# Attention and two mixtures on one core: a shorter lead of the maxima and earlier products with v in the opening

## The chip, the cores and the metric

The kernel runs on one core of a Trainium2 chip. The metric is the device time of one execution in microseconds, from the runs' times; a profile of one execution shows where that time goes. Engines are called TensorE (PE in the rows; PEld is its weight load), VectorE (DVE), ScalarE (ACT), GpSimd (POOL) and SyncE (SP, which issues DMAs).

## What is computed

Two batches of eight heads with 768 positions and 64 columns each. The scores of a pair of positions count only where both fall into the same of 64 buckets, given by the signs of six projections.

```python
q_bits = (np.einsum('bhsd,dk->bhsk', q, proj) > 0)
k_bits = (np.einsum('bhsd,dk->bhsk', k, proj) > 0)
mask = q_bucket[:, :, :, None] == k_bucket[:, :, None, :]
scores = np.where(mask, scale * np.matmul(q, k.transpose(0, 1, 3, 2)), -1e9)
scores = scores - np.max(scores, axis=-1, keepdims=True)
attn = np.exp(scores); attn = attn / (np.sum(attn, axis=-1, keepdims=True) + 1e-09)
return np.matmul(attn, v)
```

The result goes through a first mixture (1536 tokens, 512 columns, 2048 inner) and a second one with eight experts, one of which is chosen for each token. The change touches the attention only.

## The kernel before

Sixteen heads are taken one after the other, numbered 0 to 15 across both batches. For each head k and q are split into a high and a low f16 part ("hi" on ScalarE, "lo" on VectorE, or on GpSimd for heads 2 and 3), turned into the tile "tx" (keys and queries with columns on the partitions), projected (`args`, tile "ar"), and the signs written as "bits" beside a copy of the high part ("dup") into the tile "kq", which is turned in its turn into "tm". Heads 0 to 3 are turned by TensorE: twelve transposes into two PSUM buffers (`turn_pe`, tiles "psx0/1", "psm0/1"), and two copies `cx0`, `cx1` or `cm0`, `cm1` by ScalarE or VectorE (letters a, d). From head 4 on SP's transposing DMAs do that (`turn_in`).

A head's row maxima come before its scores. `max_unit` multiplies a query tile of 128 rows with 512 keys (c=0) or two query tiles with the other 256 keys (c=1) into one PSUM buffer "ms", and VectorE reduces it (lines 411 and 412, 415 and 416); nine such units make a head. `max_end` (lines 424, 425) joins them. For heads 0 to 3 `rows_t` turns the result by six small transposes into "tm" in PSUM, and `rows_in` copies it as a row into the operand of the scores (line 436).

A score unit (`score_unit`, lines 451 and 453) handles one key tile of 128 keys against 768 queries: two matmuls on tx, then two on tm, which needs the row of maxima. ScalarE takes the exponential into "p" (line 456). The products with v (`pv`) run in two halves for each key tile, in float32 (line 478) or, for the key tiles 2 and 5 of heads from 2 on, as three f16 matmuls (line 471). `out` copies the sum out.

PSUM is divided in three pools of two buffers each: ps_s for scores, ps_o for the sums of pv (and some early operands), and ps_m for everything else: ms, ar, tm, psx and psm from key tile 0 on, "tpe" (the turned expert embedding), and one buffer of the first mixture at the end. A buffer is given to the next tile when the last reader of its tile is done.

`run_all` writes the order out by hand; every engine follows the program's order. A list `PRO` gives the prologue. Then a loop goes over key tiles g from G0 = -2 to 101, with six positions in each. Score unit t of head n stands at g = 6n + t; its pv follows PVL = 3 key tiles later; the maxima lead by MXL = 10 key tiles, three units for each two key tiles. In the opening S0 and O0 give the key tiles of head 0's score units and pv. The table AT places the other steps by positions relative to the head's first key tile, AT3 those of head 3. At the end of each key tile `hook(g)` issues a share of the first mixture's preparation: weight loads on SP from g = -2, their conversion from key tile 5 on ("cv" on VectorE, then ScalarE and GpSimd), the embedding's steps ("emb": tpe at the end of key tile 11, its copy "enT" at the end of 12).

In the opening before, TensorE has in this order: head 0's row, score 0, two maxima of head 1, head 2's turned operand (into ps_o), score 1, four maxima, score 2, maxima, head 3's turned operand, and head 0's pv only in key tile 2, after the fifth score unit; head 1's maxima are complete one key tile earlier and head 2's begin in the same one.

Of the kernel before, what the change touches and what calls it, by code (L numbers as in the profile page):

```python
# [22 lines left out]
NJ = S // P  # L23
# [17 lines left out]
AT = dict(rows_t=-7, rows_in=-7, m_row=-22, bits=-90, max_end=-25, hi=-150, lo0=-127, lo1=-122, dup=-114, in_x=-116, in_m=-84, args=-91, load_kq=-182, load_v=-37, out0=50, out1=54, s_row=55, inv=77, r_out=79, r_in=91, scale=116, v16=18, p16=(9, 13), xhi=127, xlo=139)  # L41
# [6 lines left out]
SP, MP, OP = 1, (1, 5, 11), (1, 5)  # L48
# [3 lines left out]
XAT = 1, 9  # L52
TX, NX = (1, 3), {(14, 3): 0, (15, 1): 1, (15, 3): 0}
NPE = 4
AT3 = dict(x=-105, cx0=-105, cx1=-104, args=-94, m=-76, cm0=-75, cm1=-75, bits=-93, dup=-117)
CP3 = ("dd", "ad")
PVL, MXL = 3, 10
DUPE = "a"
G0 = -2
S0, O0 = (None, None, -1, 1, 2, 3), (2, 3, 4, 5, 7, 8)  # L60
PRO = """
hi 0 0
hi 0 1
# [59 lines left out]
bits 2  # L123
bits 2
score_unit 0 0
max_unit 1 0 0
hi 4
max_unit 1 1 0
m 2 o
score_unit 0 1  # L130
cm 2 1 d
cm 2 0 a
max_unit 1 1 1
""".split("\n")[1:-1]
KQW, NATW = 768, 832

# [13 lines left out]
class Attn:  # L150
# [396 lines left out]
    def run_all(self, bs, hook=None):  # L547

        seq = [(b, h) for b in bs for h in range(H)]
        N = len(seq)  # L550

        self.load_kq(0, 2)
        self.load_v(0, 0)
        act, dve = self.nc.scalar.copy, self.nc.vector.tensor_copy
        Z, pools, copies, its = self.Z, dict(s=self.ps_s, o=self.ps_o, m=self.ps_m), dict(a=act, d=dve), {}
        for line in PRO:
            f, *x = line.split()
            b, h = seq[int(x[0])] if x and f[:4] != "warm" else (0, 0)
            if f == "warm":
                self.warm(int(x[0]))  # L560
            elif f == "warm_s":
                self.warm(int(x[0]), self.ps_s.tile([P, 2, 512], F32, tag="s", name="warmed")[:, 0, 0:HS])
            elif f == "proj":
                self.proj()
            elif f == "kq":
                self.load_kq(b, h)
            elif f in ("x", "m"):
                (self.out_x if f == "x" else self.out_m)(b, h, self.turn_pe, pools[x[1]], x[1])
            elif f in ("cx", "cm"):
                Z[b, h][f](int(x[1]), copies[x[2]])  # L570
            elif f == "dup":
                self.dup(b, h, copies[x[1]])
            elif f == "args":
                self.args(b, h, pools["o"] if x[1] == "o" else None, *(int(y) for y in x[2:]))
            elif f in ("bits", "max_end"):
                if (f, h) not in its:
                    its[f, h] = getattr(self, f)(b, h)
                next(its[f, h], None)
            else:
                getattr(self, f)(b, h, *(int(y) for y in x[1:]))  # L580
        todo = {}

        def put(n, at, f, *args):
            todo.setdefault(n * NJ * 6 + at, []).append(partial(f, *seq[n], *args))

        def steps(n, f, *ats):
            def one(b, h):
                it.append(it.pop() if it else f(b, h))
                next(it[0], None)

            it = []
            for at in ats:
                put(n, at, one)

        for n in range(N):
            for name, at in AT.items():
                if n == 3:
                    at = AT3.get(name, at)
                if n == N - 1 and name in LAST:
                    continue  # L600
                if n < FROM.get(name, 0) or n >= UNTIL.get(name, N) or n % EVERY.get(name, (1, 0))[0] != EVERY.get(name, (1, 0))[1]:
                    continue
                if name == "p16":
                    for t in T16:
                        for u in range(2):
                            put(n, 6 * t + at[u], self.p16, t, u)
                elif name in GAP:
                    d = GAP[name]
                    steps(n, getattr(self, name), *(at + i * d for i in range(STEPS[name])))
                elif name == "dup":  # L610
                    put(n, at, self.dup, copies[DUPE])
                elif name in ("lo0", "lo1"):
                    put(n, at, self.lo, int(name[2]))
                elif name in ("in_x", "in_m"):
                    put(n, at, self.turn_in, name[3])
                else:
                    put(n, at, getattr(self, name))
        put(N - 2, XAT[0], self.extra)
        for n, t in NX:
            put(n, 6 * t + XAT[1], self.px, t)  # L620
        for k, f in (("x", self.out_x), ("m", self.out_m)):
            put(3, AT3[k], f, self.turn_pe, self.ps_m, "m")
            for i in range(2):
                copy = copies[CP3[k == "m"][i]]
                put(3, AT3[f"c{k}{i}"], lambda b, h, k, i, copy: Z[b, h]["c" + k](i, copy), k, i, copy)
        put(3, AT3["dup"], self.dup, dve)
        for g in range(G0, TEND + 1):
            n, t = divmod(g, NJ)
            m, j = divmod(g + MXL, NJ)
            p, u = divmod(g - PVL, NJ)  # L630
            if g < NJ:
                n, t = (0, S0.index(g)) if g in S0 else (-1, 0)
            if g < PVL + NJ:
                p, u = (0, O0.index(g)) if g in O0 else (-1, 0)
            for pos in range(6):
                first = g >= NJ + PVL and 0 <= p < N and u == NJ - 1
                if pos == SP and first:
                    self.pv(*seq[p], u, 0)
                    self.out(*seq[p], 0)
                if pos == SP and 0 <= n < N and not first:  # L640
                    self.score_unit(*seq[n], t)
                late = g == NJ - 1 and pos == OP[1]
                if late:
                    self.pv(*seq[p], u, 1)
                if 0 <= m < N and j % 2 * 6 + pos in MP:
                    i = MP.index(j % 2 * 6 + pos)
                    self.max_unit(*seq[m], j // 2 * 2 + (i > 0), int(i == 2))
                if pos == SP and 0 <= n < N and first:
                    self.score_unit(*seq[n], t)
                if pos in OP and 0 <= p < N and not (first and pos == OP[0]) and not late:  # L650
                    self.pv(*seq[p], u, OP.index(pos))
                for f in todo.get(6 * g + pos, ()):
                    f()
            if hook:
                hook(g)
# [849 lines left out]
```

## Time and profile before

| | us |
|---|---|
| median of 3 runs | 672.34 |
| lowest, highest | 672.31, 672.40 |
| profiled execution | 672.12 |
| span of the profiled execution, first to last instruction | 670.3 |
| TensorE busy in the span | 654.1 |
| VectorE, ScalarE busy | 467.5, 481.7 |

The profile is of one execution, and times in the rows are microseconds from the start of its span. A busy TensorE counts each matmul from its start to the modelled end, which includes draining. The clock granted to TensorE was 0.995 of full speed in the mean.

### The profile page before, as it was taken

To read this page: it belongs to the slowest core of one execution; us is meant where nothing else is said; L and a number is where in the kernel's file an instruction comes from. 1 tells how busy PE (TensorE), PEld (TensorE's weight loads), DVE (VectorE), ACT (ScalarE), POOL (GpSimd) and SP (SyncE) were. 2 spreads that over 40 slices of the span, in tenths; PEclk is the share of its full clock that TensorE was granted. 3 is DMA by queue.
4 is the path that set the end of the run, shared out by engine and by line. 5 is a ranking of instruction groups with operands and counts; after the bars stand their busy time and mean duration, and the time that the engine had idled before them with its cause. 6 is when DMAs were issued, how large, how long until landed. Compare 5 with 4: busy or idle time off the path is not lost.

```text
span 670.3 us, 10658 instructions
## 1 busy us (share of the span) xinstructions
PE 654.1 (98%) x3947; PEld 376.5 (56%) x3947; DVE 467.5 (70%) x795; ACT 481.7 (72%) x731; POOL 173.8 (26%) x244
## 2 busy tenths in 40 slices
PE   7999999999999999999999999999999999999994
PEld 4555555556555544444444544445477777667772
DVE  7867899999998868899655565545565765556620
ACT  6567788788776888889999788987754665555530
POOL 4023033122223422232353242532431011101111
PEclk9999999999999999999999999999999999999998
DMA  8155677977753323349033030310446988987500
GB/s 246 40 137 147 149 184 132 226 150 161 161 123 88 88 64 103 110 116 278 0 98 91 1 127 24 75 28 1 162 175 196 340 251 268 271 245 256 172 24 22
DMA packets 118429, 92.72 MB, mean 138 GB/s; under 512 B 85444, under 2 KB 97732, under 8 KB 118370
## 3 DMA queue, kind: packets, MB, share of 16 engines
q1 hardware_dynamic: 110242, 80.65, 45.0%
q0 software_dynamic: 2240, 6.31, 2.8%
q10 hardware_dynamic: 5888, 5.01, 2.4%
q8 instruction: 33, 0.54, 0.4%
q14 instruction: 26, 0.21, 0.1%
HBM read 63.44 MB, written 14.24 MB: 116 GB/s over the span
## 4 chain that ended last, share of the span: by engine, by line
PE 85%; DVE 8%; ACT 3%; issue 1%; DMA 1%; POOL 0%; POOLq 0%; ACTq 0%; DVEq 0%
PE x L930 15%; PE h L871 14%; PE y L1273 12%; PE h L1259 12%; PE o L478 11%; PE s L453 4%; PE s L451 4%; PE o L471 4%; PE ms L411 3%; PE ms L415 1%; DVE mx L412 1%; DVE cv L799 1%; PE ar L319 1%; DVE w L974 1%; DVE mx L416 1%
## 5 line engine op out<-in xcount | busy, mean ns | idle before, releaser
L871 PE MATMUL h<-xx,wi 128*128 128x512 f16 x576 | 131.3, 379 | 0.4 <-DVE w L956 0.3
L930 PE MATMUL x<-wo,g 128*128 128x512 f16 x576 | 131.2, 379 | 0.0
L478 PE MATMUL o<-p,vn 128*65 128x384 f32 (+3 forms) x260 | 104.3, 486 | 0.4 <-DVE su L503 0.4
L456 ACT ACTIVATE p<-s 128x768 f32<-128x768 f32 x96 | 77.2, 807 | 34.0 <-PE s L453 33.1
L930 PEld LDWEIGHTS <-g 128*128 128x128 f16 x576 | 56.2, 98 | 68.1 <-POOL g L968 0.8
L871 PEld LDWEIGHTS <-wi 128*128 128x128 f16 x576 | 56.0, 98 | 67.5 <-issue 0.9
L968 POOL TENSOR_TENSOR g<-w,g 128x512 f16<-128x512 f32 x47 | 57.4, 1221 | 135.4 <-ACT g L967 85.6
L1273 PE MATMUL y<-b,hh 128*128 128x512 f16 (+1 forms) x384 | 84.2, 379 | 0.0
L1259 PEld LDWEIGHTS <-a 128*128 128x128 f16 x768 | 75.1, 98 | 5.1 <-issue 0.2
L412 DVE TENSOR_REDUCE mx<-ms 128x1 f32<-128x512 f32 x96 | 64.9, 687 | 10.0 <-PE ms L411 9.3
L1259 PE MATMUL h<-xt,a 128*128 128x240 f16 x672 | 70.0, 266 | 0.0
L974 DVE SCALAR_TENSOR_TENSOR w<-w,u 128x512 f32<-128x512 f32 x47 | 34.4, 733 | 49.0 <-ACT u L965 46.8
L1273 PEld LDWEIGHTS <-hh 128*128 128x128 f16 (+1 forms) x384 | 43.7, 114 | 37.6
L951 DVE SCALAR_TENSOR_TENSOR t<-t,u 128x512 f32<-128x512 f32 x47 | 33.7, 718 | 28.8 <-ACT t L980 28.8
L1283 POOL DMA_INDIRECT out_dram<-o,row x16 | 16.5, 1034 | 142.6 <-ACT o L1280 98.8
L745 DVE SCALAR_TENSOR_TENSOR b<-st,b 128x1024 f16<-128x1024 f32 x28 | 33.1, 1222 | 25.5 <-ACT b L744 25.5
L478 PEld LDWEIGHTS o<-p,vn 128*65 128x65 f32 (+1 forms) x260 | 40.2, 163 | 16.2 <-issue 6.9
L745 DVE SCALAR_TENSOR_TENSOR a<-st,a 128x1024 f16<-128x1024 f32 x28 | 34.3, 1225 | 20.6 <-ACT a L744 20.6
L453 PE MATMUL s<-tm 97*128 97x384 f16 x192 | 47.0, 325 | 0.2 <-DVE tm L436 0.2
L451 PE MATMUL s<-tx 128*128 128x384 f16 x192 | 46.8, 325 | 0.0
L1280 ACT ACTIVATE o<-y,row 128x512 f32<-128x512 f32 (+2 forms) x16 | 10.8, 672 | 44.1 <-PE y L1273 28.2
L1265 ACT ACTIVATE hh<-h 128x480 f16<-128x480 f32 x32 | 18.2, 570 | 33.1 <-PE h L1259 30.3
(218 smaller groups left out, 1081.5 us busy)
## 6 DMA issues: line engine op xcount, KB each, us to landing
st<-in_moe_w_dram SPq DMA_DIRECT2D x32, 1024.0 KB, 5.5
stg<-in_moe_w_in_dram SPq DMA_DIRECT2D x16, 512.0 KB, 5.0
stg<-in_moe_w_out_dram SPq DMA_DIRECT2D x16, 512.0 KB, 4.2
xs<-zrow SPq DMA_DIRECT2D x15, 257.0 KB, 5.9
vn<-in_v_dram SPq DMA_DIRECT2D x16, 192.0 KB, 5.5
rb<-rd SPq DMA_DIRECT2D x14, 192.0 KB, 4.5
xr<-row SPq DMA_DIRECT2D x2, 1024.0 KB, 5.6
kq<-in_k_dram ACTq DMA_DIRECT2D x5, 384.0 KB, 5.4
```

The costliest lines, as they stand in the source:

```text
L412: nc.vector.tensor_reduce(z["mx"][:, j, 0:1], s, axis=AX.X, op=ALU.max)
L451: nc.tensor.matmul(s[:, c, :], kq[:, 0, ts], kq[:, 1, c * HS : (c + 1) * HS], start=True, stop=False)
L453: nc.tensor.matmul(s[:, c, :], m[0:97, 0, ts], m[0:97, 1, c * HS : (c + 1) * HS], start=False, stop=True)
L456: nc.scalar.activation(p[:, 0:S].rearrange("p (c n) -> p c n", c=2), s, AF.Exp, scale=2.0**-11)
L478: nc.tensor.matmul(o, self.vn(b, h, t), z["p"][t][:, cs], start=(t == 0), stop=(t == NJ - 1))
L745: nc.vector.scalar_tensor_tensor(lo, src, sc, hi, op0=ALU.mult, op1=ALU.subtract)
L871: self.nc.tensor.matmul(h, self.wi[wu][:, k, fs], x[:, k, xs], start=(i == 0), stop=(i == 3 * NKT - 1))
L930: nc.tensor.matmul(x2[r], gf[:, gu, rs], self.wo[wu][:, f, :], start=(f == 0 and gu + wu == 0), stop=(f == NF1 - 1 and gu == 1))
L968: nc.gpsimd.tensor_tensor(g[G - 1][:, 1, :], p1, g[G - 1][:, 0, :], op=ALU.subtract)
L974: nc.vector.scalar_tensor_tensor(w, w, 1.0, u, op0=ALU.add, op1=ALU.mult)
L1259: nc.tensor.matmul(h[:, v, :], W[0][wu][:, k, fs], xt[e][:, xu * NKT + k, :], start=(i == 0), stop=(i == 3 * NKT - 1))
L1273: nc.tensor.matmul(y[s][0 : CS[s].stop - CS[s].start], hs[F // 2][:, hu, F % 2, CS[s]], W[1][wu][:, F, :], start=(F == 0 and hu + wu == 0) ...
```

## The change

The lead of the maxima falls from ten to eight key tiles. Where MXL gave unit j of head m at g = 6m + j - 10, a list of the units of heads 1 to 15 is now taken from, one for each key tile from g = -2 on and two in the key tiles 12 and 17 (TWO), after which the lead is ten again. Head 0's six score units stand at prologue, prologue, -2, -1, 0 and 1 in place of prologue, prologue, -1, 1, 2 and 3, and its pv at -2, -1, 1, 3, 5 and 7 in place of 2, 3, 4, 5, 7 and 8. Head 2's operand tm is turned in key tile 2 through ps_m, not in the prologue through ps_o; head 3's goes from key tile 4 to key tile 8. The steps of `max_end` move to 13 positions ahead of heads 1 and 2, and 19 ahead of head 3.

```diff
-AT3 = dict(x=-105, cx0=-105, cx1=-104, args=-94, m=-76, cm0=-75, cm1=-75, bits=-93, dup=-117)
+AT3 = dict(x=-105, cx0=-105, cx1=-104, args=-94, m=-58, cm0=-57, cm1=-57, bits=-93, dup=-117, max_end=-19)
+AT12 = dict(max_end=-13)
-PVL, MXL = 3, 10
+PVL, TWO = 3, (12, 17)
-S0, O0 = (None, None, -1, 1, 2, 3), (2, 3, 4, 5, 7, 8)
+S0, O0 = (None, None, -2, -1, 0, 1), (-2, -1, 1, 3, 5, 7)
@@ PRO
 score_unit 0 0
-max_unit 1 0 0
-hi 4
-max_unit 1 1 0
-m 2 o
 score_unit 0 1
-cm 2 1 d
-cm 2 0 a
-max_unit 1 1 1
@@ run_all
-                if n == 3:
-                    at = AT3.get(name, at)
+                at = (AT12 if n < 3 else AT3 if n == 3 else AT).get(name, at)
...
-        for k, f in (("x", self.out_x), ("m", self.out_m)):
-            put(3, AT3[k], f, self.turn_pe, self.ps_m, "m")
+        for n, k, f in ((3, "x", self.out_x), (2, "m", self.out_m), (3, "m", self.out_m)):
+            put(n, AT3[k], f, self.turn_pe, self.ps_m, "m")
...
-                put(3, AT3[f"c{k}{i}"], lambda b, h, k, i, copy: Z[b, h]["c" + k](i, copy), k, i, copy)
+                put(n, AT3[f"c{k}{i}"], lambda b, h, k, i, copy: Z[b, h]["c" + k](i, copy), k, i, copy)
+        maxima = [(m, j) for m in range(1, N) for j in range(NJ)]
         for g in range(G0, TEND + 1):
             n, t = divmod(g, NJ)
-            m, j = divmod(g + MXL, NJ)
+            mj = [maxima.pop(0) for _ in range(1 + (g in TWO)) if maxima]
...
-                if 0 <= m < N and j % 2 * 6 + pos in MP:
-                    i = MP.index(j % 2 * 6 + pos)
-                    self.max_unit(*seq[m], j // 2 * 2 + (i > 0), int(i == 2))
+                for m, j in mj:
+                    if j % 2 * 6 + pos in MP:
+                        i = MP.index(j % 2 * 6 + pos)
+                        self.max_unit(*seq[m], j // 2 * 2 + (i > 0), int(i == 2))
```

Written out, the new order is this. A number stands for the head; "max" is one maximum unit, "pv a" and "pv b" the two halves of a product; steps of other engines are given where they read a buffer of ps_m or stand between such steps on VectorE; "cv" is the weight conversion at the key tile's end.

```
end of PRO: row of 0, score 0, score 1
-2: score 2; max 1; 0 pv a; dup 3 (VectorE); max 1; 0 pv b
-1: hi 4 (ScalarE); score 3; 0 pv a; max 1; 0 pv b
 0: score 4; max 1; psx0, psx1 of 3 (copies on VectorE); max 1
 1: score 5; 0 pv a; max 1; 0 pv b
 2: max 1; ar of 3; psm0, psm1 of 2; bits 3; cm0 (ScalarE), cm1 (VectorE); bits 3; max 1; bits 3; lo 4
 3: 0 pv a; lo 4; max 1; 0 pv b; max_end 1
 4: max 2; max 2; row of 1
 5: dup 4, hi 5 (ScalarE); 0 pv a, b; max 2; cv
 6: 1 score 0; max 2; max 2
 7: 1 score 1; 0 pv a; max 2; 0 pv b; cv
 8: 1 score 2; max 2; out of 0 (ScalarE); psm0, psm1 of 3; cm0, cm1; max 2; ar of 4; lo 5; cv
 9: bits 4; 1 score 3; 1 pv a; bits 4; lo 5; max 2; 1 pv b; max_end 2; cv
10: 1 score 4; max 3; 1 pv a; max 3; 1 pv b; row of 2
11: dup 5, hi 6 (ScalarE); 1 score 5; 1 pv a; max 3; 1 pv b; tpe; cv
12: 2 score 0; max 3; 1 pv a; max 3; max 3; 1 pv b; enT (VectorE); cv
13: 2 score 1; max 3; 1 pv a; max 3; 1 pv b
14: 1 pv a; out of 1; 2 score 2; max 3; 1 pv b; max_end 3; ar of 5; lo 6; cv
15: bits 5; 2 score 3; max 4; 2 pv a; bits 5; lo 6; max 4; 2 pv b; cv
16: 2 score 4; 2 pv a; low part of p (VectorE); max 4; 2 pv b; row of 3
17: 2 score 5; max 4; 2 pv a; max 4; max 4; 2 pv b; cv
```

From key tile 18 on the order is that of before.

## Rows read from the trace of the kernel before

**Rows 1.** The page: TensorE's share, and the chain that ended last by engine.
```profile
PE 654.1 (98%) x3947; PEld 376.5 (56%) x3947; DVE 467.5 (70%) x795; ACT 481.7 (72%) x731; POOL 173.8 (26%) x244
...
PE 85%; DVE 8%; ACT 3%; issue 1%; DMA 1%; POOL 0%; POOLq 0%; ACTq 0%; DVEq 0%
```

**Rows 2.** Table by stretch: length, busy us per engine, clock, DMA share, GB/s.
```profile
17.40:25.00 7.60, 6.11 (x49) 3.64 (x48) 6.94 (x14) 5.93 (x10) 0.28 (x1) 1.00 0.05 16
25.00:36.40 11.40, 11.23 (x74) 5.84 (x73) 8.11 (x18) 5.66 (x8) 0.90 (x1) 1.00 0.41 83
36.40:46.70 10.30, 10.30 (x60) 5.49 (x59) 9.07 (x21) 4.86 (x7) 3.45 (x3) 1.00 0.36 97
```

**Rows 3.** Timeline of TensorE, opening: start, us, engine, line, operation, idle before.
```profile
18.14 0.48 PE L453 MATMUL s<-tm 97*128 97x384 f16 x2 [0.22 <-DVE tm L436]
...
21.39 0.38 PE L411 MATMUL ms<-tm 96*128 96x512 f16 x1 [0.57 <-DVE mx L416]
...
22.96 0.38 PE L411 MATMUL ms<-tm 96*128 96x512 f16 x1 [0.32 <-DVE mx L412]
23.56 1.09 PE L253 MATMUL psx<-ident,ka 128*128 128x128 f16 x12 [0.22 <-DVE mx L416]
24.70 0.38 PE L411 MATMUL ms<-tm 96*128 96x512 f16 x1
24.92 0.49 PE L451 MATMUL s<-tx 128*128 128x384 f16 x2
...
25.57 0.38 PE L415 MATMUL ms<-tm 96*128 96x256 f16 x2
...
26.66 0.81 PE L478 MATMUL o<-p,vn 128*65 128x384 f32 x2
27.31 0.45 PE L319 MATMUL ar<-pj,tx 128*128 128x18 f16 x12
```

**Rows 4.** Timeline of TensorE, later stretches.
```profile
33.71 0.83 PE L253 MATMUL psm<-ident,kq 128*128 128x128 f16 x12
34.38 0.81 PE L478 MATMUL o<-p,vn 128*65 128x385 f32 x2
35.19 0.38 PE L415 MATMUL ms<-tm 96*128 96x256 f16 x2
...
36.39 0.59 PE L411 MATMUL ms<-tm 96*128 96x512 f16 x2 [0.17 <-ACT tm L255]
...
49.97 0.38 PE L411 MATMUL ms<-tm 96*128 96x512 f16 x1
...
51.13 0.38 PE L411 MATMUL ms<-tm 96*128 96x512 f16 x1
...
84.39 0.45 PE L319 MATMUL ar<-pj,tx 128*128 128x18 f16 x12 [0.49 <-DVE mx L412]
```

**Rows 5.** Timeline of VectorE, the same columns.
```profile
20.65 0.69 DVE L416 TENSOR_REDUCE mx<-ms 128x2 f32<-128x512 f32 x1
...
29.03 1.02 DVE L291 SCALAR_TENSOR_TENSOR ka<-kq,ka 128x384 f16<-128x384 f32 x2
...
50.38 0.69 DVE L412 TENSOR_REDUCE mx<-ms 128x1 f32<-128x512 f32 x1 [0.62 <-PE ms L411]
...
52.15 0.18 DVE L854 COPY enT<-tpe 128x64 f16<-128x64 f16 x1
```

**Rows 6.** Timeline of ScalarE, the same columns.
```profile
18.67 0.81 ACT L456 ACTIVATE p<-s 128x768 f32<-128x768 f32 x1 [0.40 <-PE s L453]
...
35.54 0.80 ACT L255 COPY tm<-psm 128x768 f16<-128x768 f16 x1
```

**Rows 7.** Waits of TensorE, whole span: total us, times, longest.
```profile
PE o L478 <- DVE su L503: 0.4, 1, 0.4
...
PE h L871 <- DVE w L956: 0.3, 1, 0.3
```

**Rows 8.** DMA issues from 25 to 60 us: count, median us to landing.
```profile
tx<-ka SPq DMA_TRANSPOSE x3, 3.8
```

## The prediction, made before the changed kernel ran

> **What bounds the kernel now.** I read first the totals of the engines: TensorE is busy 98% of the span and the chain that ended last is 85% TensorE [rows 1]. A kernel like that gains or loses time where TensorE stands still. Then the table by stretch [rows 2]: from 25 us on TensorE is nearly full in every stretch, while in the opening, from 17.40 to 25.00 us, it is busy for 6.11 of 7.60 us and VectorE for 6.94. So in that stretch VectorE sets the pace, and the change is aimed there. Third, TensorE's own timeline there [rows 3] and further on [rows 4], with VectorE's and ScalarE's beside it [rows 5, 6].
>
> A busy share hides part of a wait, because a matmul's record includes the time in which it drains. I therefore count issue time, the distance between starts in an unbroken run: 0.65 us for a score unit (24.92 to 25.57), 0.22 for a maximum's matmul (24.70 to 24.92; its record of 0.38 holds 0.16 of draining), 0.65 for one half of a product with v (26.66 to 27.31), 0.67 for twelve transposes (33.71 to 34.38) and 0.30 for the projections "ar" (0.45 less the draining) [rows 3, 4]. What exceeds this between two starts is a wait; where the row shows idle time, the wait is that and the 0.16.
>
> **How a wait comes about.** Each maximum, projection, "tm" row and half of a transposed operand takes one of two PSUM buffers of the pool ps_m and holds it until VectorE or ScalarE has read it. The case to learn from: the matmul at 49.97 ends 0.38 later, its reduction starts at 50.38 and lasts 0.69, and the next maximum starts at 51.13 in the same buffer, because the other one is held by "tpe" until its copy at 52.15 [rows 4, 5]. One buffer turns round in 1.16 us. TensorE runs in the order of the program, so everything behind such a matmul waits too, products and scores included. Two allocations in a row cost nothing; the third needs 1.16 us of other work since the first, or it waits.
>
> **Part 1: what goes.** The waits of before from the first score on are 0.39 (score, for the tm row), 0.72 (at 21.39), 0.49 (22.96), 0.38 (23.56) and 0.47 (inside the twelve transposes that take 1.14 in place of 0.67) [rows 3], then 0.12 (the projections at 27.31 end late), 0.16 (35.19), 0.32 (36.39) and 0.29 (51.13) [rows 4]. That is 3.34 us. Only the first is sure to remain: the first score unit doesn't move. The greatest possible gain is 2.95 us.
>
> **Part 2: the new order.** The amount of work is unchanged: the same matmuls, reductions and copies, and the listing shows the lead made up by two doubled key tiles, 12 and 17, after which the orders are equal. So only waits count. I carry TensorE's, VectorE's and ScalarE's queues forward in the new order, with these durations and 0.05 us from the end of a reader to the start of the matmul that waited for it (reduction at 20.65, and 0.69, makes 21.34; matmul at 21.39) [rows 3, 5].
>
> Key tiles -2 to 1. The three scores come at once, and the third needs the buffer that the first exponential (18.67 + 0.81 = 19.48) frees [rows 6]: it could start at 19.13, so 0.40 of wait. Then maxima and products alternate and no maximum waits. In key tile 0 there is no product: the second half of head 3's transposes waits for the reduction of the maximum just ahead (0.60), and the next maximum for the copy of the first half (0.20). TensorE reaches the end of key tile 1 at 28.8 us with 0.39 + 0.40 + 0.60 + 0.20 = 1.59 of waits, where before had 2.57 up to the same time. To here the change gains 1.0 us.
>
> Key tile 2. Neither a score nor a product lies in it; it has five allocations in a row: maximum, ar, two halves of head 2's operand (which before took two buffers of another pool), maximum. They wait 0.07 for a reduction, 0.57 for the next one, 0.04 for the reading of ar, and the last 0.70 for ScalarE's copy, which takes 0.80 [rows 6]. Sum 1.38.
>
> Key tiles 3 and 4. VectorE now has in one run the late maximum, the end of the bits, the two "lo" parts of head 4 (1.02 for two), the last maximum of head 1, the two small steps of its end and head 2's first maximum [rows 5]. By my count the last maximum of head 1 is reduced at 34.1 and head 2's first at 35.1, while TensorE has nothing left but maxima and the tm row from 33.3 on: 0.84 and 0.77, sum 1.61.
>
> Key tiles 6 and 8. In 6 it waits 0.07. In 8 a score and then five allocations: 0.60 for the second half of head 3's operand and 0.82 for the maximum behind it, as ScalarE has an exponential and an output copy ahead of its copy. Sum 1.49.
>
> Key tiles 9 to 17. The tm row of head 2 waits 0.42 for head 3's first maximum, which stands behind maximum end and weight work on VectorE. Then tpe holds one buffer through key tile 12, as before; but 12 is now a doubled tile, with three maxima on the one that is left: 0.29 for the second, as before, and 0.94 for the third, which follows the second at once. In 15 it is 0.05, in 17 (doubled too) 0.26. Sum 1.96.
>
> The new waits are 1.59 + 1.38 + 1.61 + 1.49 + 1.96 = 8.03 us, against 3.34: **+4.7 us**. From key tile 18 on nothing differs, and TensorE's remaining waits (0.49 and the draining at 84.39 [rows 4], 0.4 and 0.3 later [rows 7]) follow operations that move with TensorE, so I let the shift stand to the end. What could absorb it is at most those 0.65 + 0.4 + 0.3, some 1.3 us.
>
> What else moves costs nothing. SP's transposing load of head 4 waits for "lo", which I count done at 33.5 us; it lands 3.8 us after issue [rows 8] and is read by the projections in key tile 8, by my count at 43.6. The loads of v behind it on SP serve head 2, whose products begin in key tile 15. The three weight loads and the emb loads are issued by the call at the end of key tile -2, wait for nothing of TensorE's, and the weights are first read in key tile 5. On ScalarE head 4's "hi" goes behind the third exponential, and its readers are the lo's at 32.5. POOL's steps depend on key tiles far behind.
>
> Here the Trainium skill bears on the case (Perfetto Trace Analysis, Optimization Strategy): repeating gaps on the engine that should be full can mean that there isn't enough PSUM for the next tile to be allocated. The trace agrees at 51.13, with its 0.29 us. By that rule clustering allocations of one pool, as key tiles 2, 4, 8 and 12 do, is the thing to avoid.
>
> **The rivals.** (a) The gain of the opening without the later cost: the two buffers hide the readers after key tile 1, because score and product work lies close by. For it: before, from 36.40 to 46.70, TensorE is busy throughout with the same two buffers [rows 2]. Then only the later waits of before remain, and the time falls by 1.0 us (later waits as before) to 2.95 us (none but the first): 671.3 to 669.4. It decides in key tiles 2, 4 and 8: their allocations must not wait more than about 0.3 each. Against it: in 2 there is 1.4 us of TensorE work in all, and five turns of two buffers. The skill has a rule for it (Perfetto Trace Analysis, Matmuls): let independent groups rotate through different banks, so that reading one overlaps the next group's matmuls. Taken without a count of the turns it gives this rival's 669.4; the trace agrees with it only where products lie between.
>
> (b) The readers catch up in part: VectorE's late order in tiles 3 and 4 is better than I count (1.61 falls to nothing), or tpe doesn't hold its buffer (0.94 falls away), and 0.5 is absorbed later. Then +1.6 to +3.0 us: 673.9 to 675.3.
>
> (c) No change that can be seen: the moves don't reach the bound, since gain and loss cancel at about 1 us each (the 1.0 of the opening against key tile 2 alone). 671.0 to 673.6.
>
> **How the numbers follow.** The sum is made against the profiled execution: 672.12 us, of which 670.3 are the span and 1.8 lie around it; the median of the runs is 672.34, 0.2 above. 672.3 + 4.7 = 677.0. The forecast's own range goes from 3.0 (above which rival b ends) to 6.0 us (each of the seven waits of over 0.5 us longer by 0.2, the spread of my start times): 675.3 to 678.4. Chances: forecast 0.70, (b) 0.17, (c) 0.06, (a) 0.07; of (a) one part in six is a gain of less than 1.34 us. 0.2%, or 1.34 us, is about what a measurement of this kernel can tell from no change: slower by more 0.86, within 0.08, faster by more 0.06. The range reaches down through rival (b) to 673.9 and up to 678.4; what is left out is (a), (c) and a tail above.
>
> **What would show it.** TensorE should wait for ScalarE's copies (lines 255) and reductions (412, 416) between 29 and 36 us, with some 3 us of idle time there; TensorE should be a microsecond ahead of before at 28.8 us by its work, and about 4.7 behind from key tile 18 on. Three maxima in key tile 12 should start about 1.16 us apart. I am wrong if TensorE runs without a gap from 29 to 45 us, or if matmuls of the same order start earlier than in before from then on.

## The result, and the profile after

The changed kernel takes 677.53 us (median of 6 runs, 677.17 to 677.87) against 672.37 for the kernel before in the same comparison (671.80 to 672.83, 6 runs): 1.0075 times, with a 95% interval from 1.0065 to 1.0086. That is 5.2 us slower; 677.0 was predicted. The profiled execution took 677.17 us with a span of 675.4. Line numbers of the attention are six lower than before: 405 for 411, 409 for 415, 445 for 451, 472 for 478.

First the table by stretch of the changed kernel, beside [rows 2]; the columns are the same.

```profile
17.40:25.00 7.60, 7.13 (x38) 3.56 (x36) 3.12 (x7) 4.89 (x7) 0.28 (x1) 1.00 0.04 14
25.00:36.40 11.40, 8.67 (x68) 4.78 (x66) 8.51 (x18) 3.65 (x6) 0.59 (x1) 1.00 0.15 29
36.40:46.70 10.30, 9.33 (x65) 5.32 (x64) 7.60 (x17) 6.42 (x10) 1.33 (x2) 1.00 0.45 124
```

The first stretch is better than before: TensorE is busy for 7.13 us in place of 6.11, and VectorE, which was the bound there with 6.94, has only 3.12 to do. In the second TensorE loses 2.6 us (8.67 against 11.23), in the third 1.0. The gain is where the change was aimed; the loss stands behind it.

Then TensorE's timeline of the changed kernel, the rows with the longer waits and the first score of head 3 (start, us, engine, line, operation, idle before). They answer to [rows 3] and [rows 4].

```profile
19.68 0.48 PE L445 MATMUL s<-tx 128*128 128x384 f16 x2 [0.24 <-ACT p L450]
...
26.05 0.49 PE L247 MATMUL psx<-ident,ka 128*128 128x128 f16 x6 [0.44 <-DVE mx L406]
26.51 0.38 PE L405 MATMUL ms<-tm 96*128 96x512 f16 x1
...
29.19 0.45 PE L313 MATMUL ar<-pj,tx 128*128 128x18 f16 x12
30.06 0.83 PE L247 MATMUL psm<-ident,kq 128*128 128x128 f16 x12 [0.42 <-DVE mx L406]
31.44 0.38 PE L405 MATMUL ms<-tm 96*128 96x512 f16 x1 [0.55 <-ACT tm L249]
...
34.24 0.38 PE L405 MATMUL ms<-tm 96*128 96x512 f16 x1 [0.69 <-DVE mx L410]
35.24 0.49 PE L426 MATMUL tm<-ident,m 128*1 128x128 f16 x6 [0.62 <-DVE mx L406]
...
42.37 0.49 PE L247 MATMUL psm<-ident,kq 128*128 128x128 f16 x6 [0.44 <-DVE mx L406]
43.39 0.38 PE L405 MATMUL ms<-tm 96*128 96x512 f16 x1 [0.52 <-ACT tm L249]
...
49.67 0.49 PE L426 MATMUL tm<-ident,m 128*1 128x128 f16 x6 [1.03 <-DVE mx L406]
...
54.48 0.38 PE L405 MATMUL ms<-tm 96*128 96x512 f16 x1
55.64 0.38 PE L409 MATMUL ms<-tm 96*128 96x256 f16 x2 [0.78 <-DVE mx L406]
...
68.26 0.38 PE L409 MATMUL ms<-tm 96*128 96x256 f16 x2
...
68.97 0.49 PE L445 MATMUL s<-tx 128*128 128x384 f16 x2
```

Every releaser that these rows name is a reader of ps_m (a reduction on 406 or 410, or ScalarE's copy on 249), except for the third score. The last row is the first of key tile 18, from which on both kernels have the same order. In the kernel before it is this one:

```profile
63.78 0.49 PE L451 MATMUL s<-tx 128*128 128x384 f16 x2
```

The two are 5.19 us apart. Of this 0.16 lies ahead of head 0's first score, which starts at 17.42 before and at 17.58 after though the order up to it is the same; 5.03 lies between the two scores. Behind key tile 18 nothing is lost or given back on TensorE: its last matmul ends at 661.88 before and at 667.05 after, 5.17 us later.

### The profile page after: what moved, and what is told of

Its sections match the earlier page's. It is cut to its first block, busy times and chain, and to the rows that moved or that the text cites. A ratio compares the mean times of both kernels' runs of the same rounds, so it can differ in the third digit from the quotient of the medians.

```text
span 675.4 us, 10657 instructions
## 1 busy us (share of the span) xinstructions
PE 655.1 (97%) x3947; PEld 377.0 (56%) x3947; DVE 468.2 (69%) x795; ACT 480.9 (71%) x730; POOL 173.8 (26%) x244
## 4 chain that ended last, share of the span: by engine, by line
PE 84%; DVE 8%; ACT 4%; issue 1%; DMA 1%; POOL 0%; POOLq 0%; ACTq 0%; DVEq 0%
PE x L925 15%; PE h L866 14%; PE y L1268 12%; PE h L1254 12%; PE o L472 11%; PE s L445 4%; PE s L447 4%; PE o L465 3%; PE ms L405 3%; DVE mx L406 1%; PE ms L409 1%; DVE w L969 1%; DVE cv L794 1%; PE ar L313 1%; DVE cv L773 1%
## 5 line engine op out<-in xcount | busy, mean ns | idle before, releaser
L410 DVE TENSOR_REDUCE mx<-ms 128x2 f32<-128x512 f32 x48 | 33.0, 687 | 12.8 <-PE ms L409 12.2
```

## The experiments

Two theories were to be told apart. By the first, TensorE's waits are those of the two ps_m buffers for their readers, paid one for one at the place where allocations stand close together. By the second, VectorE's amount of work sets the pace of the opening, and the place doesn't matter. For each kernel the table gives two starts from its profile, those of head 0's first score and of the first matmul of key tile 18. Between these two all kernels do the same work, but for the reductions that the dose kernels add on VectorE. The order ahead of the first score is the same in all, and its start still varies from 17.35 to 17.99 us; so the distance between the two is the better measure. Behind it stands the median time, with the ratio to the kernel before in the same comparison (672.36 to 672.50 us).

| kernel | first score, us | key tile 18, us | between, us | median, us | ratio, 95% interval |
|---|---|---|---|---|---|
| before | 17.42 | 63.78 | 46.36 | 672.37 |  |
| changed | 17.58 | 68.97 | 51.39 | 677.53 | 1.0075 (1.0065 to 1.0086) |
| m2_prologue | 17.99 | 68.30 | 50.31 | 676.40 | 1.0055 (1.0039 to 1.0072) |
| two_13 | 17.59 | 68.14 | 50.55 | 676.68 | 1.0062 (1.0045 to 1.0079) |
| dose_tile_m1 | 17.58 | 68.97 | 51.39 | 677.65 | 1.0078 (1.0061 to 1.0094) |
| dose_tile3 | 17.61 | 69.72 | 52.11 | 679.75 | 1.0109 (1.0092 to 1.0126) |
| dose_tile3_again | 17.59 | 71.31 | 53.72 | 679.71 | 1.0106 (1.0088 to 1.0123) |
| dose2_tile3 | 17.60 | 72.04 | 54.44 | 680.30 | 1.0106 (1.0091 to 1.0122) |
| early_pv_only | 17.68 | 65.31 | 47.63 | 673.67 | 1.0015 (1.0006 to 1.0025) |
| lead_only | 17.35 | 65.80 | 48.45 | 674.71 | 1.0032 (1.0021 to 1.0044) |
| emb_early | 17.54 | 67.90 | 50.36 | 676.80 | 1.0067 (1.0051 to 1.0082) |
| spread_a | 17.59 | 62.78 | 45.19 | 671.29 | 0.9984 (0.9975 to 0.9993) |
| spread_c | 17.72 | 63.06 | 45.34 | 671.84 | 0.9986 (0.9977 to 0.9995) |
| spread_d | 17.59 | 62.20 | 44.61 | 670.79 | 0.9973 (0.9963 to 0.9984) |

**Fewer allocations in key tile 2 (m2_prologue).**

```diff
 score_unit 0 0
+m 2 o
 score_unit 0 1
+cm 2 0 d
+cm 2 1 d
...
-        for n, k, f in ((3, "x", self.out_x), (2, "m", self.out_m), (3, "m", self.out_m)):
+        for n, k, f in ((3, "x", self.out_x), (3, "m", self.out_m)):
```

> The changed kernel, but head 2's operand is turned in the prologue again, between the first two scores, through ps_o, with both copies on VectorE. Theory (turns of the two ps_m buffers set TensorE's waits): key tile 2 falls from five allocations to three; its waits fall from 0.07 + 0.57 + 0.71 to about 0.08 + 0.56, and the transposes fill the 0.40 us for which the third score waited. Together about 1.1 us less: 676.4 us against 677.5. Rival (VectorE's amount of work sets the pace of the opening, wherever it stands): the copies only move, one of them even from ScalarE to VectorE, so the time stays at 677.5 or rises by up to 0.5.

Measured: 676.40 us, 1.1 less than the changed kernel, and 1.08 less between the two scores. The third score follows at once (20.39, where the second starts at 19.74), and TensorE's timeline of this kernel has one wait in key tile 2 where there were two of over half a microsecond:

```profile
29.90 0.45 PE L316 MATMUL ar<-pj,tx 128*128 128x18 f16 x12
30.77 0.38 PE L408 MATMUL ms<-tm 96*128 96x512 f16 x1 [0.42 <-DVE mx L409]
```

VectorE has more to do here, not less, and the kernel is faster. That speaks against the second theory.

**The doubled key tile moved off tpe (two_13).**

```diff
-PVL, TWO = 3, (12, 17)
+PVL, TWO = 3, (13, 17)
```

> The changed kernel, but the doubled key tile 12 is 13, behind the copy that frees the buffer held by tpe. Theory: the maximum that waited 0.94 us in key tile 12 (start 55.64) is gone from there, and about 0.1 comes up in key tile 13: 0.85 us less, 676.7 us. Rival (the number of maxima behind, or VectorE, sets it): the wait moves with the doubled tile, and the time stays at 677.5.

Measured: 676.68 us, 0.85 less; between the two scores it is 0.84. The maxima of key tiles 12 and 13 in this kernel:

```profile
53.33 0.38 PE L405 MATMUL ms<-tm 96*128 96x512 f16 x1
...
54.49 0.38 PE L405 MATMUL ms<-tm 96*128 96x512 f16 x1
...
56.00 0.38 PE L405 MATMUL ms<-tm 96*128 96x512 f16 x1
...
56.87 0.38 PE L409 MATMUL ms<-tm 96*128 96x256 f16 x2
57.20 0.38 PE L405 MATMUL ms<-tm 96*128 96x512 f16 x1
```

The pair in key tile 12 still starts 1.16 us apart, one turn of the one buffer that tpe leaves. The pair in 13 (56.87, 57.20), with both buffers, is 0.33 apart. The doubling itself costs 0.1; doubling beside a held buffer costs 0.94.

**The same extra reduction at two places (dose_tile3, dose_tile_m1).** In the second kernel the number 5 is 1.

```diff
-            nc.vector.tensor_reduce(z["mx"][:, j - 1 : j + 1, 1], ...)
+            for _ in range(2 if (b, h, j) == (0, 1, 5) else 1):
+                nc.vector.tensor_reduce(z["mx"][:, j - 1 : j + 1, 1], ...)
```

> The changed kernel with the reduction of head 1's last maximum (key tile 3) done twice: one more VectorE instruction of 0.69 us, 0.60 in a run, with the same result. Theory: TensorE in key tile 4 waits for exactly this reader and what follows it on VectorE, so the time rises by 0.60 us, to 678.1. Rival (TensorE's waits of the opening are given back later): it stays at 677.5.

> The same extra reduction, but of head 1's first maximum over the last 256 keys, in key tile -1, where VectorE stands idle for 0.8 us behind it. Theory: the next maximum takes the other buffer, so nothing waits: less than 0.1 us, 677.5. Rival (VectorE's amount of work in the opening sets the pace): 0.60 us, 678.1, as in key tile 3.

Measured: 677.65 us with the reduction in key tile -1 and 679.75 (1.0109 times before, 1.0092 to 1.0126) with it in key tile 3. VectorE of dose_tile_m1:

```profile
23.78 1.42 DVE L411 TENSOR_REDUCE mx<-ms 128x2 f32<-128x512 f32 x2 [1.48 <-PE ms L409]
25.30 0.69 DVE L406 TENSOR_REDUCE mx<-ms 128x1 f32<-128x512 f32 x1
```

The work fits into idle time: the median is 0.1 us higher, within the spread, and key tile 18 starts at 68.97 as in the changed kernel. The second theory falls with this. In key tile 3 the profiled execution of dose_tile3 (678.47 us) shows the wait behind the reader longer by what was added, 1.42 in place of 0.69, and the later rows up to key tile 18 0.75 late:

```profile
34.99 0.39 PE L405 MATMUL ms<-tm 96*128 96x512 f16 x1 [1.42 <-DVE mx L411]
```

But the median rose by 2.2, three times as much as that. The theory had the place right and missed 1.4 us.

**What the other 1.4 us are (dose_tile3_again, dose2_tile3).** The same kernel on another occasion, and one with `range(3 if ...)`.

> dose_tile3 once more, on another occasion. Theory (one for one, the rest a matter of that occasion): 678.1 to 678.3. Rival (the rest belongs to this program): 679.75 again.

> The changed kernel with the reduction of head 1's last maximum done three times. With one extra reduction every matmul behind it came 0.75 us later to the end of the profiled execution, but the median time rose by 2.2. Theory (the wait behind this reader is paid one for one, and what the times show above it has to do with something else, not with the order): TensorE's matmuls come 1.4 to 1.5 us later than in the changed kernel, and the time is 678.9 plus what the second reduction adds of that unknown, 0 to 1.5. Rival (each extra reduction costs 2.2 in the time): 681.9.

Measured: 679.71 us (1.0106 times before, 1.0088 to 1.0123) and 680.30 (1.0106, 1.0091 to 1.0122). So the excess is no matter of the occasion; my expectation for the repeated run was wrong. Nor is it paid for each reduction: the second one adds 0.6 to the median, and in the profile of dose2_tile3 head 1's row starts at 36.71, 1.47 us later than in the changed kernel, as the theory had it. The profile of dose_tile3_again, this time of an execution of 679.51 us, shows where it lies. Its table by stretch, with the granted clock as the third number from the right:

```profile
33.40:36.50 3.10, 1.08 (x9) 0.59 (x9) 3.00 (x7) 0.00 (x1) 0.00 (x0) 1.00 0.55 103
36.50:37.00 0.50, 0.50 (x2) 0.27 (x3) 0.01 (x1) 0.50 (x1) 0.00 (x0) 0.81 0.84 160
37.00:40.00 3.00, 3.00 (x8) 1.12 (x7) 0.69 (x2) 1.86 (x3) 0.00 (x0) 0.50 0.91 233
40.00:40.50 0.50, 0.50 (x3) 0.25 (x2) 0.33 (x1) 0.01 (x1) 0.00 (x0) 0.78 1.10 372
40.50:44.00 3.50, 3.50 (x22) 1.92 (x21) 2.62 (x5) 1.80 (x3) 0.00 (x0) 1.00 0.23 82
```

and one stretch of the first profile of the same kernel:

```profile
37.00:40.00 3.00, 3.00 (x16) 1.57 (x15) 1.82 (x4) 2.70 (x5) 0.00 (x0) 1.00 0.91 237
```

From 33.40 to 36.50 TensorE worked for 1.08 of 3.10 us. Right behind that the granted clock stood at 0.50, the lower of its two levels (1.2 GHz), from 37 to 40 us, and TensorE did 8 matmuls there in place of 16. In the first profile, with the same 1.08 us of work in the same stretch, the clock stayed at 1.00. So the same program runs at either level after the gap. Key tile 18 starts 1.59 us later with the fall (71.31 against 69.72), and the times of the two profiled executions differ by 1.0 us (679.51 and 678.47). The runs of both occasions lie in two groups, 678.44 and 678.47, and 679.5 to 680.9. Those of dose2_tile3 do so too, 678.87 and 680.23 to 680.41; the profile is of the slowest of them and shows the same fall, from about 38 to 41 us. The faster groups lie near where one reduction (678.25, the changed kernel's 677.53 and 0.72) and two (678.97) put them without a fall. That the fall is what separates all the slower runs is likely, not shown: only three of these executions have a profile. The changed kernel's own profile has 1.00 in every stretch from 17.40 to 70 us, so its 5.2 us are waits and not clock.

**Each part alone (early_pv_only, lead_only).** The first is the kernel before with the new scores and products, the second the changed kernel with the old ones.

```diff
-S0, O0 = (None, None, -1, 1, 2, 3), (2, 3, 4, 5, 7, 8)
+S0, O0 = (None, None, -2, -1, 0, 1), (-2, -1, 1, 3, 5, 7)
```

> The kernel before with one part of the change alone: head 0's scores and products at the key tiles of the changed kernel (-2 to 1, and -2, -1, 1, 3, 5, 7); the maxima keep their lead of ten, the operands their places, and four maxima stay in the prologue between the first two scores. Theory: key tiles 2 to 4 lose their products, so allocations stand side by side there. Carrying the queues forward gives waits of 0.73 (a maximum of key tile 2), 0.85 and 0.38 (key tile 4) and 0.84 (the projections of key tile 8): 1.5 us slower than before, 673.9. Rival (early products alone are good and the shorter lead is what costs): 1 us faster, 671.4.

> The changed kernel with the scores and products of head 0 where the kernel before has them; the shorter lead, the doubled key tiles and the moved operands stay. Theory: waits of some 1.3 us around head 3's operand in key tile 0 come back, those of key tile 4 go, and those of key tiles 2 (0.7), 8 (0.8), 12 (1.2) and 17 (0.24) remain: 1.8 us slower than before, 674.2, so that the two parts alone (1.5 and 1.8) make less than the 5.1 of both. Rival (costs add up, the shorter lead makes all of it): 5 us slower or more, 677.5.

Measured: 673.67 us, 1.3 slower than before (1.27 between the two scores), and 674.71, 2.3 slower (2.09). Both rivals fall: early products alone are no gain, and the shorter lead alone makes less than half of the loss. The four waits of early_pv_only that were expected:

```profile
31.21 0.38 PE L411 MATMUL ms<-tm 96*128 96x512 f16 x1 [0.55 <-DVE mx L412]
...
34.01 0.38 PE L411 MATMUL ms<-tm 96*128 96x512 f16 x1 [0.69 <-DVE mx L416]
34.61 0.49 PE L432 MATMUL tm<-ident,m 128*1 128x128 f16 x6 [0.22 <-DVE mx L412]
...
42.90 0.45 PE L319 MATMUL ar<-pj,tx 128*128 128x18 f16 x12 [0.65 <-DVE mx L412]
```

With the draining added they are 0.71, 0.85, 0.38 and 0.81. In lead_only:

```profile
27.11 0.38 PE L405 MATMUL ms<-tm 96*128 96x512 f16 x1 [0.27 <-ACT tm L249]
...
40.22 0.38 PE L405 MATMUL ms<-tm 96*128 96x512 f16 x1 [0.59 <-ACT tm L249]
...
46.51 0.49 PE L426 MATMUL tm<-ident,m 128*1 128x128 f16 x6 [0.41 <-DVE mx L406]
...
52.48 0.38 PE L409 MATMUL ms<-tm 96*128 96x256 f16 x2 [0.78 <-DVE mx L406]
```

The row at 46.51 is head 2's, and its wait of 0.57 was not expected; it is most of the half microsecond by which lead_only misses 674.2. VectorE's second step of head 2's end takes 0.89 us there, beside GpSimd's third step for the embedding, which runs from 44.35 to 45.50:

```profile
44.63 0.89 DVE L419 TENSOR_SCALAR m<-m 128x6 f16<-128x6 f32 x1
```

The next experiment is about this pair.

Between the two scores the parts sum up to 3.36 us, both together make 5.03. The waits of the four kernels, counted as in the prediction, show where the remaining 1.7 us lie. Up to key tile 1 the kernel before waits 2.45 us, early_pv_only 1.12, lead_only 1.96 and the changed kernel 1.52: each part takes waits away there, but both together take less than the two savings added up, and that is 0.9 of the 1.7. Head 2's row waits 0.09, 0.09, 0.57 and 1.19 in the same order, which makes 0.6. The rest is smaller, at key tiles 3 to 8. In key tile 2 the costs of the two simply add up.

**GpSimd beside VectorE (emb_early).** The embedding's steps are tied to key tiles by bare `yield`s.

```diff
-        for _ in range(6):
+        for _ in range(5):
             yield
...
+        yield
         yield
         yield
         yield
         pt = ps.tile([P, 2, NKT, E0], F16, tag="m", name="tpe")
```

> The changed kernel with GpSimd's three steps for the expert embedding (1.05, 1.01 and 1.15 us, of 512 columns) issued one key tile earlier, and tpe where it was. In the changed kernel VectorE's second step of head 2's end took 0.90 us in place of 0.17, from 47.80 to 48.70, beside GpSimd's third step, which ran from 47.51 to 48.66. Theory (VectorE's step was held up by GpSimd's): the step takes 0.17 again, the row of head 2 waits some 0.45 us in place of 1.19, and the time falls by 0.7 us, to 676.8. Rival (a chance delay of that execution, or one made by VectorE's own neighbours): no change, 677.5.

Measured: 676.80 us, 0.7 less. By TensorE's rows it is more, 1.03 between the two scores, and head 2's row waits 0.19 and not the expected 0.45. (Behind TensorE's last matmul the profile has 9.0 us here and 8.35 in the changed kernel; why is open.) VectorE's second step of head 2's end, in the changed kernel and then in emb_early:

```profile
47.80 0.90 DVE L419 TENSOR_SCALAR m<-m 128x6 f16<-128x6 f32 x1
```

```profile
47.45 0.17 DVE L419 TENSOR_SCALAR m<-m 128x6 f16<-128x6 f32 x1
```

and GpSimd's third step in the changed kernel:

```profile
47.51 1.15 POOL L839 TENSOR_TENSOR en<-e,en 8x512 f16<-8x512 f32 x1
```

GpSimd's step ends at 48.66, VectorE's at 48.70. With that step out of the way VectorE's takes 0.17 again, and head 2's row, at 49.67 in the changed kernel, starts 1.07 us earlier:

```profile
48.60 0.49 PE L426 MATMUL tm<-ident,m 128*1 128x128 f16 x6
```

The 0.73 us on VectorE's step were GpSimd's. The edit does a little more than that: the two small steps of VectorE on which GpSimd's first one waits (0.13 and 0.15 us, on "ess") move to the earlier key tile as well, and with them about the rest of what the row gained.

**A version made to the theory (spread_a, spread_c, spread_d).** The core of spread_a against the changed kernel, beside the prologue of m2_prologue:

```diff
-AT3 = dict(..., m=-58, cm0=-57, cm1=-57, ..., max_end=-19)
-AT12 = dict(max_end=-13)
-PVL, TWO = 3, (12, 17)
-S0, O0 = (None, None, -2, -1, 0, 1), (-2, -1, 1, 3, 5, 7)
+AT3 = dict(..., m=-76, cm0=-75, cm1=-75, ..., max_end=-19)
+AT1, AT2 = dict(max_end=-8), dict(max_end=-13)
+PVL, TWO = 3, (14, 11)
+S0, O0 = (None, None, 0, 2, 3, 4), (-2, 0, 2, 4, 5, 8)
```

> A version made to the theory. Head 0's scores stand in the prologue (two) and in key tiles 0, 2, 3 and 4, its products in -2, 0, 2, 4, 5 and 8; the doubled key tiles are 11 and 14; head 2's operand is turned in the prologue through ps_o with copies on VectorE, head 3's in key tile 5; the ends of the maxima follow their last unit. So a score or a product lies between any three allocations of ps_m. Theory: carrying the queues forward leaves waits of 0.39, 0.47, 0.16, 0.27 and four of less than 0.1, 1.5 us in all up to key tile 18, against 3.3 in the kernel before: 1.8 to 2 us faster than before, 670.5. Rival (the kernel before has what can be had, since something else then ends last in the opening): no faster than 672.3.

Measured: 671.29 us, 0.9984 times before (0.9975 to 0.9993). It is faster than both kernels, than the one before by 1.1 us (1.17 between the two scores) and not by the 1.8 to 2 expected. What is missing is the row of head 2, whose wait I had put at nothing and which waited 0.66, draining included: VectorE's second step at the end of head 2 again lasted 0.90 us beside GpSimd's third. Two kernels move GpSimd's steps, by one key tile to either side (5 and 7 in place of 6, and tpe where it was).

> spread_a with GpSimd's three steps for the expert embedding one key tile earlier, as in emb_early. In spread_a VectorE's second step of head 2's end again took 0.90 us (42.93) beside GpSimd, and the row of head 2 waited 0.50 and the draining at 44.81. Theory (GpSimd's step held it up): 0.17, the row waits about 0.1, and the time falls by 0.5 us from spread_a's 671.29 to 670.8. Rival (in this order something else ends as late): 671.3.

> spread_a with GpSimd's three steps for the expert embedding one key tile later, so that the third of them runs beside reductions of VectorE, which read PSUM, and not beside an instruction whose operands lie in SBUF. In spread_c, with the steps a key tile earlier, another such instruction met the third step (1.64 us in place of 0.66, from 40.36 on) and the gain didn't come. Theory (VectorE's instruction is held until GpSimd's is done): the step of head 2's end takes 0.17 us, no other instruction is stretched, the row of head 2 waits less than 0.2, and the time falls by 0.5 to 0.6 us from spread_a's 671.29, to 670.7. Rival (something else ends as late): 671.3.

Measured: 671.84 us for spread_c, no better than spread_a, against my expectation. There VectorE's weight conversion came to stand beside GpSimd's third step (40.10 to 41.46) and took 1.64 us in place of 0.66:

```profile
40.10 1.36 POOL L842 TENSOR_TENSOR en<-e,en 8x512 f16<-8x512 f32 x1
```

```profile
40.36 1.64 DVE L776 SCALAR_TENSOR_TENSOR cv<-stg,cv 128x512 uint32<-128x512 uint32 x1
```

What stands behind it on VectorE came later by that, and head 2's row (45.09) still waited 0.31 and the draining.

In spread_d, where only reductions from PSUM meet that step, the time is 670.79 us, 0.9973 times before (0.9963 to 0.9984): 1.7 us faster than the kernel before (1.75 between the two scores) and 6.7 faster than the changed one. VectorE's step and head 2's row there:

```profile
42.61 0.17 DVE L422 TENSOR_SCALAR m<-m 128x6 f16<-128x6 f32 x1
```

```profile
44.22 0.49 PE L429 MATMUL tm<-ident,m 128*1 128x128 f16 x6
```

Its table by stretch shows a full TensorE from 25 us on, and an opening that is better than before:

```profile
17.40:25.00 7.60, 7.06 (x54) 4.12 (x52) 5.85 (x12) 4.79 (x8) 0.28 (x1) 1.00 0.06 20
25.00:36.40 11.40, 11.24 (x75) 5.90 (x74) 8.39 (x19) 6.33 (x8) 0.59 (x1) 1.00 0.45 97
36.40:46.70 10.30, 10.30 (x64) 5.78 (x62) 8.79 (x22) 6.08 (x9) 2.52 (x3) 1.00 0.57 128
```

The wish behind the change, products in the place of TensorE's waits in the first stretch, could be had; what it couldn't bear was to take the products out of the key tiles that follow. The spread kernels change several places at once, and how much each of them brings was not taken apart.

## Why the prediction was right, point by point

The sign, the mechanism and the size hold. The waits by the prediction's own parts, with the draining added where a row shows idle time:

| key tiles | predicted, us | measured, us |
|---|---|---|
| -2 to 1 | 1.59 | 0.39 + 0.40 + 0.61 + 0.12 = 1.52 |
| 2 | 1.38 | 0.07 + 0.57 + 0.71 = 1.35 |
| 3, 4 | 1.61 | 0.85 + 0.78 = 1.63 |
| 6, 8 | 1.49 | 0.08 + 0.60 + 0.68 = 1.36 |
| 9 to 17 | 1.96 | 1.19 + 0.29 + 0.94 + 0.24 = 2.66 |
| sum | 8.03 | 8.52 |

*What goes.* 3.34 us were counted for before. 8.52 less 3.34 is 5.18; between the two scores 5.03 were measured. The count of before leaves out 0.09 ahead of each of the rows of heads 1 and 2 (32.59 and 46.32), which the changed kernel's waits there contain; with it the two agree to 0.03. The bound of 2.95 us for any gain stood by TensorE's rows; spread_d took 1.75 of it.

*The opening gains 1.0 us.* It does: the waits up to the end of key tile 1 are 1.52, against the 2.57 of before up to the same time. The maximum of key tile 2 starts at 28.90 in the changed kernel; 28.8 was said for it.

*Key tiles 2, 4 and 8.* Their waits came within 0.14 us each, and m2_prologue and dose_tile3 show in place and size that they are waits for readers of ps_m.

*tpe and the doubled key tile.* 0.29 and 0.94, as counted from the 1.16 us of [rows 4, 5]; two_13 took the second away.

*The row of head 2* is the term that was mis-sized: 0.42 predicted, 1.19 measured. The step of the working was "which stands behind maximum end and weight work on VectorE", with durations from [rows 5] and the small steps at 0.17. In the new order GpSimd's third step met the second of them, which cost that step 0.73 us. In the kernel before the same step of GpSimd ran beside reductions from PSUM and one instruction that had begun ahead of it, so its rows didn't show this price. They hold a smaller sign of it: a step of VectorE that takes 0.20 in the median ended 0.05 us after GpSimd's first step, at 0.29.

```profile
42.42 1.05 POOL L842 TENSOR_SCALAR e<-e,ess 8x512 f32<-8x512 f32 x1 [11.92 <-DVE ess L841]
```

```profile
43.23 0.29 DVE L330 TENSOR_SCALAR kq<-ag 128x72 f16<-128x72 f32 x1
```

With GpSimd's steps out of the way (emb_early) the row waits 0.19, less than the 0.42. So the size of this term was near by neither measure. The other terms sum up to 7.61 us predicted and 7.33 measured, so the miss of 0.5 us is this row's 0.77 less 0.28.

*The shift stands to the end*, as predicted: 5.19 us at key tile 18, 5.17 at the last matmul, 5.1 in the span, 5.16 in the median. Nothing of the 1.3 us that might have been absorbed was.

*The rivals.* (a), the reading hidden behind other work, needed waits of no more than 0.3 in key tiles 2, 4 and 8; they were 0.57 to 0.85. (b) needed better times in the key tiles 3 and 4 or a free buffer beside tpe, and neither came. (c) set the opening's 1.0 us against key tile 2 alone; the key tiles behind it waited another 5.65 us, against 0.77 in the kernel before. The Trainium skill says that the same gap repeating on the engine that should be full can mean too little PSUM for the next tile (Perfetto Trace Analysis, Optimization Strategy). This trace agrees far more than the one row of before let see: eight waits of 0.57 to 0.94 us and one of 1.19, all on readers of one pool of two buffers. The Trainium skill's advice to let independent groups rotate through different banks (Perfetto Trace Analysis, Matmuls) holds in key tiles -2, -1 and 1, where maxima and products alternate and no maximum waits; in 2, 4 and 8 the same two buffers rotate, and TensorE waits.

*Two slips in the numbers.* The upper end of the range counts seven waits of over 0.5 us; the prediction's own list has eight, which makes 6.3 and not 6.0 us. The chances listed add up to 0.87 for slower and 0.07 for no change, where 0.86 and 0.08 were given. Neither bears on the outcome.

## What to carry to other kernels

Where an engine runs in program order, count the allocations of each small pool between pieces of other work: with two buffers the third allocation has to lie a full turn (here 1.16 us) behind the first, or everything behind it waits. Filling one gap with work from a later stage takes that stage's cover away, so carry the queues forward through the stage that gives, not only through the one that gets. Which instructions of two engines come to run side by side changes with any reordering; a price that the trace before doesn't show may come from that.

## What the runs showed of the hardware that was not expected

VectorE and GpSimd hold each other up. A step of VectorE on 128x6 elements took 0.90 us in place of 0.17, and ended 0.04 us after GpSimd's 1.15 us subtraction of two operands, which works on eight partitions only. In spread_c a weight conversion took 1.64 in place of 0.66 beside the same step. A reduction from PSUM beside it (44.94 in the kernel before, where that step runs from 44.64 to 46.03) kept its 0.68. The other way round, GpSimd's second step took 1.01 us in the changed kernel, where an instruction of VectorE with two operands in SBUF began at the same moment (46.41, 0.55 us), and 0.60 in emb_early, where only the end of a reduction ran beside it:

```profile
46.41 1.01 POOL L838 CAST en<-e 8x512 f16<-8x512 f32 x1
```

```profile
42.21 0.60 POOL L838 CAST en<-e 8x512 f16<-8x512 f32 x1
```

The Trainium skill (SBUF — State Buffer, Who interferes with whom) gives a reason: the two engines share one pair of ports to SBUF, an exclusive lock that whichever issues first keeps for its whole instruction; VectorE needs it in its two-port modes, which a tensor_scalar can enter, or for a second input from SBUF, and a tensor_reduce never does on trn2. The traces agree with the waiting to the end (48.70 behind 48.66) and with reductions being free of it (0.68).

TensorE's clock can fall in the middle of a full program. After a stretch in which TensorE worked 1.08 of 3.10 us, with idle times of 1.42 and 0.60 us, the granted clock stood at 0.50, its lower level, for some 3.5 us in one execution of dose_tile3's program and at 1.00 in another. In the changed kernel, with 0.69 and 0.62 us at the same place, the profiled execution kept 1.00. In this kernel the longer wait was thus paid a second time, with 1.6 us on TensorE, in some executions; the program alone doesn't tell in which.
